# The inner layer's columns dealt in pairs: longer runs for w_out, stepped weight loads for w_in

## The chip, the cores and the metric

The kernel runs on one core of one Trainium2 chip. The metric is the device time of one execution in microseconds, the median of several runs. A core has five engines that work side by side and meet through semaphores: TensorE (matmuls; its weight loads, LDWEIGHTS, are listed apart as PEld), VectorE (DVE), ScalarE (ACT), GpSimd (POOL) and SyncE (SP), which here issues nearly all DMA transfers. Data lies in HBM, is worked on in SBUF (128 partitions), and TensorE writes its sums to PSUM, of which the kernel uses eight banks of 512 float32 columns.

## What is computed

Two layers in a row, float32 in and out. The first is linear attention over 8 batches, 8 heads, 576 positions and 64 features:

```python
q_s = softmax of q over the 64 features
k_s = softmax of k over the 576 positions
kv  = einsum('bhsd,bhse->bhde', k_s, v)   # a 64 x 64 matrix for each head
out = q_s @ kv                             # (8, 8, 576, 64)
x   = out, heads side by side              # 4608 tokens x 512
```

The second is a feed-forward layer with 512 inputs, 2048 inner columns and 512 outputs:

```python
h = x @ w_in                               # w_in 512 x 2048
g = h * (1.0 / (1.0 + np.exp(-beta * h)))  # beta: one value for each of the 2048 inner columns
return g @ w_out                           # w_out 2048 x 512
```

The sum over the 2048 inner columns in the last line may be taken in any order, and it may be cut into any groups, as long as the column of w_in, the value of beta and the row of w_out that belong together meet. The change below is about how these columns are grouped.

## The kernel before

**Chunks and units.** The 4608 tokens are worked through in nine chunks of 512 tokens (`NCH = 9`); chunk 7 is made of the last positions of all batches (`TAILS`), the others of the first 512 positions of one batch. The 2048 inner columns are cut into 16 groups of 128 (`NJ = 16`). A unit `n` is one group `u = n % 16` of one chunk `c = n // 16`; there are 144 units. Each has four steps:

- `h n` (`st1`, line 889): four matmuls of TensorE, one for each 128 rows of w_in. The stationary operand (the weights) is a block of `w_in_b`, 128 x 128, and the moving one is the chunk's `xT`, 512 tokens. They add up in one PSUM bank of a ring of four, `hT`.
- `th n` (`tanh`, line 907): ScalarE takes the tanh, scaled by a column of `beta_c`, which holds one value of beta for each partition.
- `g n` (`gate`, line 924): VectorE computes (tanh + 1) * h into `g`, in bfloat16.
- `o n` (`st2`, lines 951 and 959): four matmuls, one for each 128 tokens. Here `g` is the stationary operand and row group `u` of `w_out_b` the moving one; the results add up over the 16 units of a chunk in four PSUM banks, `acc`, and are stored at its end.

The first four units are cut in halves of 256 tokens, and each half into two pieces of two matmuls (`h 0 0 0` is unit 0, first half, rows 0 and 2 of the four), so that they can start on the first half of `xT`. So the first 32 matmuls of line 889 are 256 columns wide, the others 512.

**Weights.** w_in and w_out come as float32 by DMA into four staging tiles `wst` and are cast to bfloat16 into `w_in_b` and `w_out_b`. There are eight blocks, alternately of w_in (512 of its columns) and of w_out (512 of its rows), each loaded in two halves (`ld w0 1`, `ld w0 0`, ...; `load_w`, lines 316 and 318). The staging tiles are used twice, so that the loads of blocks 4 to 7 wait for the casts of blocks 0 to 3. In a load of w_in each partition gets two runs of 512 values (2 KB), and so it does in one of w_out: row `128 j + p` goes to partition `p`. The casts (`cast_w`, which goes through the helper at lines 232 and 234) are given to ScalarE or GpSimd by the written order. The first block of w_in is cast in two pieces for each half: columns 0 to 127, which is what unit 0 needs, and columns 128 to 511. ScalarE has both pieces of half 1 and the first piece of half 0; GpSimd has the second piece of half 0.

**beta** (lines 343 to 353) is loaded as 16 rows of 128 values, turned by one transpose on TensorE into 128 x 16, and copied to `beta_c` by ScalarE.

**The order.** Every engine works through its instructions in the order in which they are written. That order is the text `ORDER` at the head of the file: 1,200-odd steps, by name, with the engine behind the name where there is a choice. The part that the change touches, the end of the start-up, reads:

```python
kv_0_1, qsum_0_2_0, kexp_0_1, kv_0_0, cast_w0_1_1=act,
qtrev_0_0_0=act, qtr_0_1_0, qmax_1_1, qtrev_0_0_1=dve, qsum_0_2_1, qmax_1_0, cast_w0_1_0=act, ld_w2_0,
qtrev_0_1_0=act, kvn_0, qnorm_0_1_1=pool, cast_w0_0_1=pool, beta_tr, beta_ev, qtr_0_1_1, qsub_1_0=pool,
cast_w0_0_0=act, x_0_0_1, x_0_0_0, qtrev_0_1_1=dve, xev_0_0_0=dve, qrcp_0_2, x_0_1_1, qnorm_0_2_0=pool,
qnorm_0_2_1=pool, xev_0_0_1=act, x_0_1_0, fill_10, fill_5, cast_w2_0=pool, ld_w2_1, xev_0_1_0=dve, ld_w1_0, ld_w1_1,
cast_w2_1=pool, h_0_0_0, h_0_0_1, h_1_0_0, h_1_0_1, h_0_1_0, xev_0_1_1=act, th_0_0, th_1_0, h_0_1_1, qmax_1_2,
```

Here `qtr` are transposes of the normalised q on TensorE, `qtrev` the copies of their results to `qT`, `kv` and `kvn` the 64 x 64 matrices and their normalisation, `x` the matmuls that give x transposed (64 x 64 tiles), `xev` the copies of it to `xT`, and `fill` matmuls whose results nobody uses. The attention of the later batches is woven between the units of the feed-forward layer in the same text. Tiles and semaphores are managed below this level: an instruction waits for those whose data it needs.

Of the kernel before, what the change touches and what calls it, by code (L numbers as in the profile page):

```python
# [9 lines left out]
F32 = mybir.dt.float32  # L10
ALU = mybir.AluOpType
ACTF = mybir.ActivationFunctionType
# [105 lines left out]
def kernel(  # L118
# [11 lines left out]
    P = 128  # L130
# [7 lines left out]
    NJ = FF // P  # L138
# [13 lines left out]
    def op(name, fn, eng=None):  # L152
        assert name not in ops, name
        ops[name] = (fn, eng)
# [4 lines left out]
    def sbt(name, shape, dt):  # L159
        return sb.tile(shape, dt, name=name)  # L160

    ident_f = sbt("ident_f", [P, P], F32)
# [2 lines left out]
    minus = sbt("minus", [P, P], F32)  # L165
    warm = sbt("warm", [P, P], BF16)
    first = sbt("first", [P, 1], F32)
    beta_rows = sbt("beta_rows", [NJ, P], F32)
    beta_c = sbt("beta_c", [P, NJ], F32)
    w_in_b = sbt("w_in_b", [P, KT, FF], BF16)  # L170
    w_out_b = sbt("w_out_b", [P, NJ, DM], BF16)
# [23 lines left out]
    th = [sbt(f"th{i}", [P, 512], BF16) for i in range(3)]  # L195
# [5 lines left out]
    place = {}  # L201
# [4 lines left out]
    def take(*who):  # L206
        assert sum(last in done for last, _ in turns) >= len(who), who
        for w in who:
            n = next(n for n, (last, _) in enumerate(turns) if last in done)
            i = turns.pop(n)[1]  # L210
            place[w] = ring[i][:]
            turns.append((w, i))

    def made(what, *parts):
        done.update((what, p) for p in parts)

    def uses(what, *parts):
        for p in parts:
            assert (what, p) in done, (what, p)
# [7 lines left out]
    dve, act, pool, pe, sp = nc.vector, nc.scalar, nc.gpsimd, nc.tensor, nc.sync  # L227
# [64 lines left out]
    for b in range(B):  # L292
        n = 2 if b else 1
# [4 lines left out]

    W = [(w, blk) for blk in range(4) for w in ("i", "o")]
    w_in_v = w_in.rearrange("(kt p) f -> p kt f", p=P)
    w_out_v = w_out.rearrange("(j p) f -> p j f", p=P)

    def load_w(n, half):
        which, blk = W[n]
        if n > 3:
            which, blk = W[n - 4]
            if which == "i":
                uses("i", *[(4 * blk + u, half) for u in range(4)])  # L310
            else:
                uses("o", 2 * blk + half)
            which, blk = W[n]
        dst = wst[n % 4][:, 2 * half : 2 * half + 2, :]
        if which == "i":
            sp.dma_start(dst, w_in_v[:, 2 * half : 2 * half + 2, 512 * blk : 512 * blk + 512])
        else:
            sp.dma_start(dst, w_out_v[:, 4 * blk + 2 * half : 4 * blk + 2 * half + 2, :])

    def cast_w(n, half, eng, c0=0, c1=512):  # L320
        which, blk = W[n]
        s = wst[n % 4][:, 2 * half : 2 * half + 2, c0:c1]
        if which == "i":
            made("i", *[(4 * blk + c // P, half) for c in range(c0, c1, P)])
            cast(eng, w_in_b[:, 2 * half : 2 * half + 2, 512 * blk + c0 : 512 * blk + c1], s)
        else:
            made("o", 2 * blk + half)
            cast(eng, w_out_b[:, 4 * blk + 2 * half : 4 * blk + 2 * half + 2, :], s)

    for n in range(8):  # L330
        for half in range(2):
            op(f"ld w{n} {half}", lambda n=n, half=half: load_w(n, half))
            if n == 0:
                for c, (c0, c1) in enumerate(((0, P), (P, 512))):
                    op(
                        f"cast w{n} {half} {c}",
                        lambda e, n=n, half=half, c0=c0, c1=c1: cast_w(n, half, e, c0, c1),
                        "pool",
                    )
            else:  # L340
                op(f"cast w{n} {half}", lambda e, n=n, half=half: cast_w(n, half, e), "pool")

    def beta_tr():
        take("beta")
        pe.transpose(place["beta"][:, 0:NJ], beta_rows[:], ident_f[0:NJ, 0:NJ])

    def beta_ev():
        done.add("beta")
        act.copy(beta_c[:], place["beta"][:, 0:NJ])

    op("ld beta", lambda: sp.dma_start(beta_rows[:], beta.rearrange("(j p) -> j p", p=P)))
    op("beta tr", beta_tr)
    op("beta ev", beta_ev)

# [427 lines left out]
    for h in range(3):  # L782
        i0, i1 = 4 * h, min(4 * h + 4, NI)
        for J in range(2):
            p = dict(j=2 * J, n=2, i0=i0, i1=i1)
# [57 lines left out]
    def chunk_x(c):  # L843
        if c == TAILS:
            return xTt
        return xT[(c if c < TAILS else c - 1) % 2]

    def halves(h):
        return (0, 1) if h is None else (h,)

    def cols(h):
        return slice(0, 512) if h is None else slice(256 * h, 256 * h + 256)
# [3 lines left out]
    def bank(n, h):  # L856
        key = ("h", n) if h is None else ("hp", n // 2, h)
        if key not in place:
            take(key)
        if h is None:  # L860
            return place[key]
        return place[key][:, 256 * (n % 2) : 256 * (n % 2) + 256]

    def turn(n, h):
        return n if h is None else 2 * (n // 2) + h

    def st1(n, ks=(0, 1, 2, 3), h=None):
        c, u = divmod(n, NJ)
        x = chunk_x(c)
        for kt in ks:  # L870
            uses("i", (u, kt // 2))
            if c == TAILS:
                uses("xTt", *[(b, kt % 2) for b in range(B)])
            else:
                uses("xT", *[(c - (c > TAILS), kt, a) for a in halves(h)])
        if h is not None and n % 2 and ks[0] == 0:
            uses("st1", (n - 1, h))
        if ks[0]:
            uses("begun", (n, h))
        made("begun", (n, h))  # L880
        w = bank(n, h)
        if c == 0 and h is None:
            w = w.rearrange("p (h c) -> p h c", h=2)
        for kt in ks:
            r = x[:, kt, cols(h)]
            if c == 0:
                r = x_first[:, kt % 2, kt // 2]
                r = r if h is None else r[:, h]
            pe.matmul(  # L889
                w,  # L890
                w_in_b[:, kt, u * P : (u + 1) * P],
                r,
                start=(kt == 0),
                stop=(kt == KT - 1),
            )
        if KT - 1 in ks:
            made("st1", *[(n, a) for a in halves(h)])

    def tanh(n, h=None):
        u = n % NJ  # L900
        mates = [n] if h is None else [2 * (n // 2), 2 * (n // 2) + 1]
        uses("st1", *[(m, a) for m in mates for a in halves(h)])
        if turn(n, h) >= 3:
            uses("gated", turn(n, h) - 3)
        made("tanh", *[(n, a) for a in halves(h)])
        c = cols(None if h is None else n % 2)
        act.activation(th[turn(n, h) % 3][:, c], bank(n, h), ACTF.Tanh, scale=beta_c[:, u : u + 1])  # L907

    def gate(n, h=None):
        mates = [n] if h is None else [n, n + 1]  # L910
# [88 lines left out]
    for n in range(NU):  # L999
        if n < LEAD:  # L1000
            for h in range(2):
                for x in range(2):
                    op(f"h {n} {h} {x}", lambda n=n, h=h, x=x: st1(n, (x, x + 2), h))
                op(f"th {n} {h}", lambda n=n, h=h: tanh(n, h))
                if n % 2 == 0:
                    op(f"g {n} {h}", lambda n=n, h=h: gate(n, h))
                op(f"o {n} {h}", lambda n=n, h=h: st2(n, h))
            continue
        if n in (16, 17):
            op(f"h {n} 0", lambda n=n: st1(n, (0, 1)))  # L1010
            op(f"h {n} 1", lambda n=n: st1(n, (2, 3)))
        else:
            op(f"h {n}", lambda n=n: st1(n))
        op(f"th {n}", lambda n=n: tanh(n))
        op(f"g {n}", lambda n=n: gate(n))
        if n >= NU - LAST:
            for t in range(3):
                op(f"o {n} {t}", lambda n=n, t=t: st2(n, ts=[t]))
            for x in range(2):
                op(f"o {n} 3 {x}", lambda n=n, x=x: st2(n, ts=[3], xs=[x]))  # L1020
        else:
            op(f"o {n}", lambda n=n: st2(n))
# [47 lines left out]
```

## Time and profile before

| | |
|---|---|
| Median of 3 runs (lowest, highest) | 287.05 us (286.97, 287.06) |
| The profiled execution: its own time, its span | 287.31 us, 285.5 us |
| Granted TensorE clock, mean | 0.999 |
| Busy: TensorE, weight loads, VectorE, ScalarE, GpSimd | 275.8, 129.9, 194.9, 174.2, 131.2 us |
| HBM read, written | 36.71 MB, 9.44 MB |
| Loads of w_in: number, size each, median from issue to landing | 8, 512 KB, 7.9 us |
| Loads of w_out: the same | 8, 512 KB, 11.2 us |

Times in the profile are in microseconds from the start of the span. An engine is busy while one of its instructions runs; a row of the profile names the line, the engine, the operation, the tile written and the tile read (`w_in_b<-wst` is a cast of weights), and the shape as partitions x elements. Matmuls are pipelined: one starts before the one ahead of it has left the array, so the length of a single matmul (some 379 ns for 512 columns) is more than the distance between two. Weight loads run beside the matmul ahead. The chain of waits is followed back from the last instruction: at each step it goes to what released it. A wait for several things is put down to the one that came last.

### The profile page before, as it was taken

What the parts mean: (1) busy time and instruction counts of PE and PEld (TensorE: products, weight loads), DVE (VectorE), ACT (ScalarE), POOL (GpSimd) and SP (SyncE); (2) the same over time, 40 slices, a digit from 0 to 9 for tenths busy, and PEclk for the clock granted to TensorE, in tenths of its full rate; (3) what the DMA queues carried; (4) which work ended last, traced back from release to release, by engine and by line L of the source; (5) the groups of instructions that cost most, each with busy time, mean ns of one, the idle gap of its engine ahead of it and who ended that gap; (6) DMA issues with size and microseconds to landing.
All of it is one profiled execution on the core that took longest, in us unless ns stands there. A gap on an engine that the chain in (4) does not pass through costs nothing.

```text
span 285.5 us, 5163 instructions
## 1 busy us (share of the span) xinstructions
PE 275.8 (97%) x1947; PEld 129.9 (45%) x1977; DVE 194.9 (68%) x394; ACT 174.2 (61%) x291; POOL 131.2 (46%) x93
## 2 busy tenths in 40 slices
PE   7799999999999999999999999999999999999994
PEld 2356544444444544444444544444444444444442
DVE  2998957999899898997667858555754263435421
ACT  2498885887488577837586566564671274345422
POOL 6899996869379948083960650090020000000000
PEclk9999999999999999999999999999999999999999
DMA  7999999990991994991434927000054001005104
GB/s 229 390 391 385 384 389 391 390 336 7 276 371 43 316 275 181 295 329 41 152 119 113 189 62 193 0 3 2 0 141 164 0 0 39 0 0 187 73 0 147
DMA packets 37048, 50.01 MB, mean 175 GB/s; under 512 B 15760, under 2 KB 16160, under 8 KB 37024
## 3 DMA queue, kind: packets, MB, share of 16 engines
q1 hardware_dynamic: 36880, 49.63, 53.4%
q8 instruction: 15, 0.25, 0.3%
q10 hardware_dynamic: 144, 0.07, 0.1%
q14 instruction: 9, 0.07, 0.1%
HBM read 36.71 MB, written 9.44 MB: 162 GB/s over the span
## 4 chain that ended last, share of the span: by engine, by line
PE 91%; DMA 4%; ACT 1%; SPq 1%; issue 1%; DVE 0%
PE hT L889 43%; PE acc L959 42%; DMA kf<-in_k_dram 2%; DMA wst<-in_moe_w_in_dram 2%; PE hT L638 2%; PE hT L688 1%; SPq L275 1%; PE hT L951 1%; PE acc L951 1%; ACT w_in_b L232 0%; PE hT L464 0%; PE hT L734 0%; ACT qT L232 0%; ACT ek L612 0%; ACT ek L605 0%
## 5 line engine op out<-in xcount | busy, mean ns | idle before, releaser
L907 ACT ACTIVATE th<-hT,beta_c 128x512 bf16<-128x512 f32 (+1 forms) x148 | 96.6, 677 | 66.9 <-PE hT L889 48.5
L924 DVE SCALAR_TENSOR_TENSOR g<-th,hT 128x512 bf16<-128x512 bf16 x144 | 94.6, 680 | 58.5 <-ACT th L907 55.5
L959 PE MATMUL acc<-w_out_b,g 128*128 128x512 bf16 x543 | 130.7, 379 | 1.4 <-issue 0.8
L889 PE MATMUL hT<-xT,w_in_b 128*128 128x512 bf16 (+1 forms) x517 | 117.7, 372 | 0.7 <-issue 0.2
L889 PEld LDWEIGHTS <-w_in_b 128*128 128x128 bf16 x592 | 57.6, 98 | 64.8 <-ACT w_in_b L232 0.2
L959 PEld LDWEIGHTS <-g 128*128 128x128 bf16 x560 | 53.7, 98 | 64.5 <-issue 2.9
L560 POOL TENSOR_TENSOR kf<-kf,kmb 128x1152 f32<-128x1152 f32 (+1 forms) x15 | 38.0, 2543 | 23.6 <-DVE kmb L550 17.6
L441 POOL TENSOR_TENSOR qn<-eqe,qz 128x1152 bf16<-128x1152 bf16 (+2 forms) x20 | 34.5, 1739 | 28.0 <-DVE qz L433 18.1
L393 POOL TENSOR_TENSOR qf<-qf,qm 128x1152 f32<-128x1152 f32 (+2 forms) x20 | 34.4, 1733 | 18.4 <-issue 11.9
L378 DVE TENSOR_REDUCE qm<-qf 128x9 f32<-128x576 f32 (+2 forms) x34 | 23.3, 704 | 6.2 <-DMA qf<-in_q_dram 6.2
L422 ACT ACTIVATE eqe<-qf 128x576 bf16<-128x576 f32 (+2 forms) x34 | 21.5, 657 | 9.5 <-POOL qf L393 9.5
L232 ACT CAST xT<-hT 128x512 bf16<-128x512 f32 x19 | 12.6, 740 | 21.1 <-PE hT L688 21.1
L428 DVE TENSOR_REDUCE qs<-eqe 128x9 f32<-128x585 bf16 (+2 forms) x34 | 24.0, 713 | 0.5 <-ACT eqe L422 0.4
L490 DVE TRANSPOSE_TENSOR_REDUCE km<-kf 128x18 f32<-128x576 f32 x32 | 23.6, 754 | 0.0
L612 ACT ACTIVATE ek<-kf 128x576 bf16<-128x576 f32 x30 | 19.5, 683 | 0.9 <-DMA vf<-in_v_dram 0.9
L234 POOL CAST va<-vf 128x1152 bf16<-128x1152 f32 (+1 forms) x11 | 12.0, 1105 | 6.9 <-DMA vf<-in_v_dram 6.9
L889 PE MATMUL hT<-xTt,w_in_b 128*128 128x512 bf16 x63 | 14.9, 379 | 0.1
L234 DVE CAST xT<-hT 128x512 bf16<-128x512 f32 x9 | 6.3, 728 | 7.0 <-PE hT L688 7.0
L232 ACT COPY osb<-acc 128x512 f32<-128x512 f32 x14 | 7.8, 594 | 3.0 <-PE acc L959 3.0
L367 PE MATMUL hT<-g,warm 128*128 128x512 bf16 x21 | 7.0, 482 | 1.6 <-POOL g L240 1.5
L234 DVE COPY osb<-acc 128x512 f32<-128x512 f32 (+1 forms) x6 | 3.8, 632 | 4.9 <-PE acc L951 3.8
L638 PEld LDWEIGHTS <-ek 64*64 64x64 bf16 x576 | 5.7, 106 | 2.2 <-issue 1.3
(74 smaller groups left out, 121.7 us busy)
## 6 DMA issues: line engine op xcount, KB each, us to landing
qf<-in_q_dram SPq DMA_DIRECT2D x14, 576.0 KB, 6.9
kf<-in_k_dram SPq DMA_DIRECT2D x14, 576.0 KB, 7.7
vf<-in_v_dram SPq DMA_DIRECT2D x14, 576.0 KB, 8.4
out_dram<-osb SPq DMA_DIRECT2D x19, 256.0 KB, 2.6
wst<-in_moe_w_in_dram SPq DMA_DIRECT2D x8, 512.0 KB, 7.9
wst<-in_moe_w_out_dram SPq DMA_DIRECT2D x8, 512.0 KB, 11.2
out_dram<-wst SPq DMA_DIRECT2D x16, 256.0 KB, 3.7
qf<-in_q_dram SPq DMA_DIRECT2D x4, 288.0 KB, 4.1
```

What stands on the lines that cost most here:

```text
L234: eng.tensor_copy(dst, src)
L378: dve.tensor_reduce(qm[:, j : j + n, i0:i1], qf[b % 2][:, j : j + n, i0:i1], axis=AX.X, op=ALU.max,)
L393: eng.tensor_tensor(x, x, m, ALU.subtract)
L422: act.activation(eq[:, i0:i1, j : j + n, :].rearrange("p i j d -> p j i d"), x, ACTF.Exp)
L428: dve.tensor_reduce(qs[:, i0:i1, j : j + n].unsqueeze(3), x, axis=AX.X, op=ALU.add)
L441: eng.tensor_tensor(qn[b % 2][:, i0:i1, j : j + n, :], eq[:, i0:i1, j : j + n, :], z, ALU.mult)
L490: dve.tensor_reduce(km[:, j : j + n].rearrange("p j i e -> p (j i e)"), kf[b % 2][:, j : j + n].rearrange("p j i (e c) -> p (j i e) c", c=32),
L560: eng.tensor_tensor(x, x, m, ALU.subtract)
L889: pe.matmul(w, w_in_b[:, kt, u * P : (u + 1) * P], r, start=(kt == 0), stop=(kt == KT - 1),)
L907: act.activation(th[turn(n, h) % 3][:, c], bank(n, h), ACTF.Tanh, scale=beta_c[:, u : u + 1])
L924: dve.scalar_tensor_tensor(out=out, in0=of, scalar=1.0, in1=src, op0=ALU.add, op1=ALU.mult)
L959: pe.matmul(acc[t][:], g[n % NG][:, t * P : (t + 1) * P], w_out_b[:, u, :], start=(u == 0), stop=(u == NJ - 1),)
```

## The change

Inner columns are dealt to the units in pairs. Two neighbouring units `2m` and `2m + 1` share the 256 columns from `256 m` on; the first takes the even ones and the second the odd ones, so that partition `p` of unit `2m + r` is column `256 m + 2 p + r`. Before, unit `u` took columns `128 u` to `128 u + 127`.

- **w_out**: rows `256 m + 2 p` and `256 m + 2 p + 1` go to the same partition and lie side by side in HBM, so that a load has one run of 4 KB for each partition in place of two of 2 KB. The tile `w_out_b` and the matmuls that read it are as before.
- **w_in**: loads and layout in SBUF are as before. The weight load of a unit now takes every second of 256 columns, a step of two elements. The two pieces of the first block are columns 0 to 255 and 256 to 511, since units 0 and 1 need the first 256.
- **beta**: loaded as 8 rows of 256 values; two transposes, one for the even and one for the odd values (read with a step of two), in place of one. `beta_c` has the even units in its first eight columns and the odd ones in the other eight, and `tanh` picks the column by `v`.

The number and order of all other instructions are the same.

```diff
-    beta_rows = sbt("beta_rows", [NJ, P], F32)
+    beta_rows = sbt("beta_rows", [NJ // 2, 2 * P], F32)
...
-    w_out_v = w_out.rearrange("(j p) f -> p j f", p=P)
+    w_out_v = w_out.rearrange("(m p r) f -> p m r f", p=P, r=2)
...
-            sp.dma_start(dst, w_out_v[:, 4 * blk + 2 * half : 4 * blk + 2 * half + 2, :])
+            sp.dma_start(dst, w_out_v[:, 2 * blk + half])
...
-                for c, (c0, c1) in enumerate(((0, P), (P, 512))):
+                for c, (c0, c1) in enumerate(((0, 2 * P), (2 * P, 512))):
...
-        pe.transpose(place["beta"][:, 0:NJ], beta_rows[:], ident_f[0:NJ, 0:NJ])
+        for r in range(2):
+            n = NJ // 2
+            pe.transpose(place["beta"][:, n * r : n * r + n], beta_rows[:, r : 2 * P : 2], ident_f[0:n, 0:n])
...
-    op("ld beta", lambda: sp.dma_start(beta_rows[:], beta.rearrange("(j p) -> j p", p=P)))
+    op("ld beta", lambda: sp.dma_start(beta_rows[:], beta.rearrange("(m q) -> m q", q=2 * P)))
...
-                w_in_b[:, kt, u * P : (u + 1) * P],
+                w_in_b[:, kt, 2 * P * (u // 2) + u % 2 : 2 * P * (u // 2) + 2 * P : 2],
...
         u = n % NJ
+        v = NJ // 2 * (u % 2) + u // 2
...
-        act.activation(th[turn(n, h) % 3][:, c], bank(n, h), ACTF.Tanh, scale=beta_c[:, u : u + 1])
+        act.activation(th[turn(n, h) % 3][:, c], bank(n, h), ACTF.Tanh, scale=beta_c[:, v : v + 1])
```

## The prediction

> **What bounds the kernel now.** I read the page first (busy shares, the chain), then the busy time of each engine over the long middle, then what TensorE waits for there, then the start-up instruction by instruction. From the page:
>
> ```profile
> PE 275.8 (97%) x1947; PEld 129.9 (45%) x1977; DVE 194.9 (68%) x394; ACT 174.2 (61%) x291; POOL 131.2 (46%) x93
> ...
> PE 91%; DMA 4%; ACT 1%; SPq 1%; issue 1%; DVE 0%
> ```
>
> TensorE is busy 275.8 of 285.5 us and holds 91% of the chain. Next, busy time by engine from the first matmul of the inner layer to 262 us (from, to, length, then busy us and instructions by engine, granted clock, share of the DMA engines, GB/s), and all waits of TensorE from 20.5 us to the end:
>
> ```profile
> 20.57:262.00 241.43, 239.37 (x1695) 111.73 (x1721) 173.71 (x346) 155.27 (x257) 114.95 (x64) 1.00 0.53 169
> ```
>
> ```profile
> PE acc L959 <- issue: 0.8, 5, 0.2
> PE hT L367 <- issue: 0.2, 1, 0.2
> PE hT L889 <- issue: 0.2, 1, 0.2
> ```
>
> In 241.43 us TensorE is idle for 2.06, at a granted clock of 1.00, and no wait is on a DMA, a cast or another engine; they are 0.2 us each, where it comes back from 64x64 tiles to full ones. So the time is three things: when the inner layer starts (20.57 us), how fast matmuls follow one another, and the end. A change counts if it moves the start or the pitch. The chain of waits, in order of time (start, length, what), shows both:
>
> ```profile
> 4.03 6.47 DMA kf<-in_k_dram
> ...
> 10.52 5.99 DMA wst<-in_moe_w_in_dram
> ...
> 17.67 0.72 ACT w_in_b L232
> 18.39 0.36 ACT qT L232
> ...
> 18.76 0.42 ACT w_in_b L232
> 19.18 0.49 ACT qT L232
> ...
> 19.72 0.41 PE acc L688 x8
> 20.13 0.16 issue
> 20.29 0.38 PE hT L367
> 20.67 7.01 PE hT L889 x48
> ...
> 37.32 3.46 PE hT L889 x16
> ```
>
> Sixteen 512-column matmuls of L889 take 3.46 us, 0.216 each. Ahead of the first one ScalarE is the chain: it alternates the first w_in casts with copies of qT. The change touches these casts.
>
> **The first w_in casts.** Two units now share 256 columns, so the first 512-column block is cut 256 + 256 in place of 128 + 384. On ScalarE the order stays: rest of half 1, qT, first part of half 1, qT, beta, first part of half 0, then the first xT copy. GpSimd has the rest of half 0. ScalarE's timeline (start, length, instruction):
>
> ```profile
> 17.56 0.83 ACT L232 CAST w_in_b<-wst 128x768 bf16<-128x768 f32 x1
> 18.28 0.59 ACT L232 COPY qT<-acc 128x512 bf16<-128x512 bf16 x1
> 18.76 0.42 ACT L232 CAST w_in_b<-wst 128x256 bf16<-128x256 f32 x1
> ...
> 19.07 0.60 ACT L232 COPY qT<-acc 128x512 bf16<-128x512 bf16 x1
> 19.54 0.20 ACT L349 COPY beta_c<-hT 128x16 f32<-128x16 f32 x1
> 19.61 0.44 ACT L232 CAST w_in_b<-wst 128x256 bf16<-128x256 f32 x1
> 19.91 0.77 ACT L232 CAST xT<-acc 128x512 bf16<-128x512 f32 x1
> ```
>
> 768 values a partition take 0.83 us and 256 take 0.42: 0.41 for 512 values, so 512 take 0.42 + 0.205 = 0.63. The first cast shrinks by 0.20, the second grows by 0.20: the qT copy of 19.07 starts when it did. The third, of 19.61, also grows, and nothing pays for it: 0.44 becomes 0.64, and the xT copy behind it moves from 19.91 to 20.12 and ends at 20.89, not 20.68. Who waits for it is TensorE's third matmul. Its rows, with VectorE's xT copy, which lets the first one go:
>
> ```profile
> 20.29 0.38 PE L367 MATMUL hT<-g,warm 128*128 128x512 bf16 x1 [0.16 <-issue]
> 20.57 0.49 PE L889 MATMUL hT<-xT,w_in_b 128*128 128x256 bf16 x3
> ```
>
> ```profile
> 19.77 0.75 DVE L234 CAST xT<-acc 128x512 bf16<-128x512 f32 x1 [0.22 <-ACT beta_c L349]
> ```
>
> VectorE ends at 20.52 and the first matmul starts at 20.57: 0.05 for the hand-over. One 256-column matmul lasts 0.27 (row below), so the third of 20.57 to 21.06 starts at 20.79. ScalarE's copy was ready for it at 20.68 + 0.05 = 20.73, 0.06 ahead. With 20.89 + 0.05 = 20.94 it starts 0.15 late. The next copy (second of its kind) then ends near 21.50, ahead of its matmul, the eleventh: 20.57 + 10 x 0.109 + 0.15 = 21.81. So the stream loses **0.15 us**, once. Bounds: 0, if the cast overlaps the copy, and 0.2, the whole growth. I take 0.15 since each link has its own row. GpSimd's 0.82 us cast of 768 shrinks by some 0.2; it moves up a chain that TensorE doesn't wait for: no gain.
>
> **beta by two transposes.** One weight load and one matmul of fp32 more:
>
> ```profile
> 18.46 0.13 PEld L345 LDWEIGHTS hT<-ident_f,beta_rows 16*128 16x128 f32 x1
> 18.62 0.17 PEld L464 LDWEIGHTS <-qn 128*128 128x128 bf16 x3
> ...
> 18.46 0.23 PE L345 MATMUL hT<-ident_f,beta_rows 16*128 16x16 f32 x1
> ```
>
> From its load to the next load is 0.16 us; that is the price of the second. Queued behind it on TensorE are four transposes, which VectorE's copy of qT waits for, and then the second x matmuls, which end at 20.13 by the chain; they move by 0.16 at most. So do the two fill matmuls behind them. The last fill could let L889 start at 20.29 + 0.22 = 20.51, and it starts at 20.57, so that 0.06 are free and the first two matmuls of L889 move by at most 0.1, still ahead of 20.94. ScalarE reads beta only at 19.54, 0.85 us after the transpose ends. Cost: 0 under the cover of the late xT copy; with that cover gone up to 0.1. The beta load (8 runs of 1 KB for 16 of 512 B) stands in SP's queue ahead of the w_in loads, which were cast from 17.56 on: it is in time.
>
> **w_in's weights with a step of two.** The main risk: 592 weight loads of L889. Rows by shape (busy us, mean ns, idle before), and from the timeline eight loads and transposes in a row, and the kv loads:
>
> ```profile
> L889 PE MATMUL hT<-xT,w_in_b 128*128 128x256 bf16 x32 | 3.7, 273 | 0.0
> ...
> L889 PEld LDWEIGHTS <-w_in_b 128*128 128x128 bf16 x592 | 57.6, 98 | 64.8 <-ACT w_in_b L232 0.2 <-issue 0.2
> ...
> L580 PEld LDWEIGHTS acc<-kf,ident_f 128*128 128x128 f32 x4 | 0.7, 188 | 1.3 <-issue 1.2
> ```
>
> ```profile
> 17.24 0.85 PEld L638 LDWEIGHTS <-ek 64*64 64x64 bf16 x72 [0.46 <-ACT ek L612]
> ...
> 31.94 0.61 PE L464 MATMUL hT<-ident,qn 128*128 128x128 bf16 x8
> ```
>
> A load takes 98 ns from start to end, under a matmul with a pitch of 216 (109 in the 32 of 256 columns). Back to back they go closer: eight transposes, each with its load, take 0.61 us, (0.61 - 0.22) / 7 = 0.056 a load. No load of before has a step, so its price is bounded: from below 0 (a load already hidden can't gain); from above by the fp32 load, 188 ns, whose 128 columns lie four bytes apart, as the stepped ones do. The 64-column loads of L638 say that even narrow ones go at 0.85 us for 18 at each of four tile positions, under 0.05 each, so 128 columns under 0.1. All of these are under 0.216, and 560 of 592 loads are hidden whichever holds. Exposed would be the 32 with a pitch of 0.109 and the three units (31, 51, 109) that the written order puts right behind 64x64 work. At 0.188: 31 x (0.188 - 0.109) = 2.4 and 3 x 0.09 = 0.3, so **+2.7 us** as the upper end. I take 0: nearest are the bf16 rows, 0.056 to 0.1, under both pitches.
>
> Here a rule speaks against the change. The Trainium skill, "TensorE: Matmul & The Clock Gate", section "Weight-path perf modes — Fast Weight Load (FWL) and DoubleRow", says that a full bf16 load reads 32 bits, two weights, at a time in four chunks, packed or stepped. By it, as an estimate, a step of two would waste half of each read; no load of before can show that. The same page's plain formula (columns / 1.2 ns) gives 107 ns, under 109. What half the rate would cost from rows is a rival below.
>
> **w_out in runs of 4 KB.** Eight loads; half as many packets each. The rows (size, median us from issue to landing), then all traffic at 14 to 17 us (nearly all w_in, runs of 2 KB) and at 44 to 56 us (q, k, v, runs of 2.25 KB):
>
> ```profile
> wst<-in_moe_w_out_dram SPq DMA_DIRECT2D x8, 512.0 KB, 11.2
> ```
>
> ```profile
> DMA packets 587, 1.17 MB, mean 391 GB/s; under 512 B 32, under 2 KB 32, under 8 KB 587
> ```
>
> ```profile
> DMA packets 2178, 4.68 MB, mean 390 GB/s; under 512 B 128, under 2 KB 128, under 8 KB 2176
> ```
>
> 391 against 390 GB/s: the queue is full and the longer run is no faster. At 390 a load of 0.52 MB is 1.34 us of the stream. Runs of 4 KB may save some of that, at most 8 x 1.34 = 10.7, likely under 1; but no TensorE wait after 20.5 is on a DMA, and the chain's DMA pieces, k and w_in, end at 16.51. The closest use is the first w_out block:
>
> ```profile
> 26.07 2.02 POOL L234 CAST w_out_b<-wst 128x1024 bf16<-128x1024 f32 x2
> ...
> 27.52 1.89 PE L959 MATMUL acc<-w_out_b,g 128*128 128x512 bf16 x7
> ```
>
> Half of it is cast at 27.08 and used at 27.52: 0.4 us of room, and GpSimd was held by its own queue, not the load. Cost and gain 0. SP's next w_in load waits for the longer cast of 19.61 and so goes out 0.2 us later, into a queue that stays full: 0. If that cover went, 0.2 more.
>
> **Sum.** +0.15 (cast) + 0 + 0 + 0 on the profiled span of 285.5: 285.65. That run took 287.31 (1.8 around the span), 0.26 above the median of 287.05; on the median, 287.05 + 0.15 = **287.20**.
>
> **Rivals.** (a) Stepped loads at half rate: 0.112 each against 0.109: 31 x 0.003 + 3 x 0.06 = 0.3, so 287.5. For it: the rule above; against: nothing measured. (b) Slower side: stepped loads as slow as fp32 ones. Place: the 32 half-width matmuls from 20.57 on. It decides from 0.109 us a load; price 2.7, so 289.9. Above 0.216 every unit would pay, 560 x the excess, for which no row speaks. (c) A cast or copy with little room (0.06 to 0.4 us) arrives late because the start-up shifts ScalarE, GpSimd and VectorE against each other: a new wait of 0.5 to 1, so 287.7 to 288.2. Against it: they follow TensorE's own shift. (d) Faster: the shorter DMA stream brings everything forward. It needs a TensorE wait on data, and there is none after 20.5; before it, at most 0.2 from the shorter first cast: 286.85. (e) Long runs change nothing in the queue, landing still near 11.2: the time is that of my sum.
>
> **Chances.** My sum, with (e): 0.72, own range 287.0 to 287.45. (a) 0.10, (b) 0.07, (c) 0.07, (d) 0.04. The range from 286.8 to 288.2 leaves out (b) and odd cases. 0.2% is 0.57 us, about what a measurement here can tell from no change: 286.48 to 287.62. Within it are my sum, nearly all of (a), and a quarter of (d): 0.82; slower: (b), (c) and 0.01 of (a), 0.15; faster: the rest of (d), 0.03, for a wait in the start-up that is worth more than I can see.
>
> **What would show it.** The third L889 matmul at 20.94, 0.15 late; the cast ahead of xT at 0.63; two loads of beta 0.1 to 0.16 apart; L889's 512-column matmuls at 0.216 still, the 256-column ones at 0.109; the w_out packets halved and no DMA wait on TensorE. Wrong if L889's weight loads rise over 109 ns with the pitch following, or a new wait of TensorE shows between 20 and 60 us.

## The result: 3% slower, and the profile after

The changed kernel takes 295.5 us (median; lowest 294.0, highest 297.53) against 287.01 before, a ratio of 1.030 (95% interval 1.024 to 1.0365). The profiled execution took 294.0 us with a span of 292.2; before it was 287.31 and 285.5. From the page of the changed kernel, the busy times, the chain and the granted clock in 40 slices of 7.3 us:

```profile
PE 277.2 (95%) x1948; PEld 130.5 (45%) x1978; DVE 195.1 (67%) x394; ACT 175.0 (60%) x291; POOL 131.1 (45%) x93
...
PEclk9999979999999999999999999999999999999999
...
PE 86%; DMA 4%; DVE 3%; issue 2%; POOL 1%; ACT 1%; SPq 1%; DVEq 0%; POOLq 0%
```

TensorE is busy for 1.4 us longer, with one matmul more on the page, and its share of the span falls from 97% to 95%; GpSimd, which was not in the chain before, has a share of it, and in one slice the granted clock falls. Whom TensorE waited for, from 18 us to the end (us in total, times, longest):

```profile
PE hT L892 <- POOL w_in_b L234: 5.6, 3, 3.2
PE acc L963 <- issue: 0.8, 5, 0.2
PE hT L892 <- issue: 0.2, 1, 0.2
PE hT L370 <- issue: 0.2, 1, 0.2
```

Three rows of before are there again. New are three waits of the inner layer's matmuls (line 892 is 889 before) for casts of w_in on GpSimd. TensorE's timeline at these places, and GpSimd's (start, length, instruction):

```profile
19.48 0.38 PE L892 MATMUL hT<-xT,w_in_b 128*128 128x256 bf16 x2
21.55 0.28 PE L892 MATMUL hT<-xT,w_in_b 128*128 128x256 bf16 x1 [1.69 <-POOL w_in_b L234]
22.54 0.72 PE L892 MATMUL hT<-xT,w_in_b 128*128 128x256 bf16 x5 [0.70 <-POOL w_in_b L234]
...
34.04 0.38 PE L892 MATMUL hT<-xT,w_in_b 128*128 128x512 bf16 x1
37.64 2.63 PE L892 MATMUL hT<-xT,w_in_b 128*128 128x512 bf16 x7 [3.22 <-POOL w_in_b L234]
40.07 1.06 PE L467 MATMUL hT<-ident,qn 128*128 128x128 bf16 x8
```

```profile
20.46 2.02 POOL L234 CAST w_in_b<-wst 128x1024 bf16<-128x1024 f32 x2
...
36.54 1.04 POOL L234 CAST w_in_b<-wst 128x1024 bf16<-128x1024 f32 x1
```

The first two matmuls of unit 0 run; the third starts when the first of GpSimd's two casts of 20.46 is through, the fourth when the second is, at 22.48. By the written order these are the casts of block 1, the columns 512 to 1023, and unit 0 reads columns 0 to 255. Unit 10 is held in the same way: its first matmul runs at 34.04, its second waits until the cast of 36.54, which is block 3, columns 1536 to 2047, has ended at 37.58; unit 10 reads 1280 to 1535. TensorE waits for data that it doesn't use, so the section on the kernel before, where an instruction waits for those whose data it needs, is not the whole truth. In the kernel before, the same cast of block 3 starts when unit 10 is already through: its four matmuls are the first of eight in a row, without a wait:

```profile
32.39 1.89 PE L889 MATMUL hT<-xT,w_in_b 128*128 128x512 bf16 x8
...
34.88 1.04 POOL L234 CAST w_in_b<-wst 128x1024 bf16<-128x1024 f32 x1
```

Behind the last wait the seven matmuls take 2.63 us, where six distances of 0.216 and one length of 0.38 make 1.68. The busy times in stretches (from, to, length, busy us by engine, then granted clock, DMA share and GB/s), of the changed kernel:

```profile
34.00:42.00 8.00, 4.78 (x24) 2.30 (x22) 4.70 (x12) 3.60 (x5) 7.31 (x6) 0.79 1.04 393
...
37.60:41.70 4.10, 4.06 (x17) 2.04 (x18) 1.24 (x3) 1.91 (x3) 3.43 (x2) 0.58 1.04 395
```

In the kernel before, the stretch from 34 to 42 has TensorE busy for 7.95 of 8.00 us at a clock of 1.00, against 4.78 at 0.79 here:

```profile
34.00:42.00 8.00, 7.95 (x44) 3.95 (x44) 5.42 (x14) 7.10 (x11) 7.30 (x5) 1.00 1.05 388
```

So the span of the profiled execution adds up. The matmul behind each wait starts 1.96, 0.99 and 3.60 us after the one ahead of it, where 0.109, 0.109 and 0.216 were due: 1.85 + 0.88 + 3.38 = 6.1 lost. The clock costs 4.10 x (1 - 0.58) = 1.7. The inner layer started at 19.48, 1.1 earlier than at 20.57 before; that start lies between 19.20 and 20.73 in the profiles of this document, so the 1.1 is not put down to the change. 6.1 + 1.7 - 1.1 = 6.7, which is 292.2 - 285.5.

The profiled execution is the fastest of the four, and the clock accounts for the others. Their spans are 292.2, 293.7, 295.7 and 293.7 us at mean granted clocks of 0.992, 0.988, 0.981 and 0.988; span times clock is 289.9, 290.2, 290.1 and 290.2.

### The profile page after: what moved, and what is told of

The parts are those of the page before. It is cut to its first block, busy times and chain, and to the rows that moved or that the text cites. A ratio compares the mean times of both kernels' runs of the same rounds, so it can differ in the third digit from the quotient of the medians.

```text
span 292.2 us, 5166 instructions
## 1 busy us (share of the span) xinstructions
PE 277.2 (95%) x1948; PEld 130.5 (45%) x1978; DVE 195.1 (67%) x394; ACT 175.0 (60%) x291; POOL 131.1 (45%) x93
## 4 chain that ended last, share of the span: by engine, by line
PE 86%; DMA 4%; DVE 3%; issue 2%; POOL 1%; ACT 1%; SPq 1%; DVEq 0%; POOLq 0%
PE hT L892 40%; PE acc L963 40%; DMA kf<-in_k_dram 3%; PE hT L641 2%; DMA qf<-in_q_dram 1%; PE hT L691 1%; DVE km L493 1%; POOL qn L444 1%; DVE qs L431 1%; PE hT L955 1%; PE acc L955 1%; PE acc L596 1%; SPq L275 1%; DVE qm L381 1%; ACT th L911 1%
## 5 line engine op out<-in xcount | busy, mean ns | idle before, releaser
L892 PE MATMUL hT<-xT,w_in_b 128*128 128x512 bf16 (+1 forms) x517 | 119.5, 375 | 6.3 <-POOL w_in_b L234 5.6
```

The costliest lines, as they stand in the source:

```text
L892: pe.matmul(w, w_in_b[:, kt, 2 * P * (u // 2) + u % 2 : 2 * P * (u // 2) + 2 * P : 2], r, start=(kt == 0), stop=(kt == KT - 1),)
```

## The experiments

Two theories that stood against each other, and a third. **W**: a stepped load is made to wait for casts of other columns, since tiles are watched for overlap, and a load with a step of two and a cast of two rows in one tile are held to overlap although they share no element. **S**: the stepped loads themselves are slow, or disturb what runs beside them. **R**: the 4 KB runs change when weights land. Intervals are of 95%.

### The same stepped loads, with w_in in several tiles

```diff
-    w_in_b = sbt("w_in_b", [P, KT, FF], BF16)
+    w_in_0 = [[sbt(f"w_in_0_{a}_{c}", [P, 2, 256], BF16) for c in range(2)] for a in range(2)]
+    w_in_t = [[sbt(f"w_in_{blk}_{a}", [P, 2, 512], BF16) for a in range(2)] for blk in range(1, 4)]
...
-                w_in_b[:, kt, 2 * P * (u // 2) + u % 2 : 2 * P * (u // 2) + 2 * P : 2],
+                w_in_of(u // 4, kt // 2, 256 * (u // 2 % 2))[:, kt % 2, u % 2 : 2 * P : 2],
```

> The changed kernel with w_in_b cut into several tiles: the first block into one tile for each half and 256 columns, the other blocks into one for each half. All 592 weight loads keep their step of two, w_out keeps its 4 KB runs, beta its two transposes. Theory W (a stepped load is made to wait for GpSimd casts of columns that it doesn't read, since casts of two rows of w_in and the stepped columns are held to overlap in one tile): no wait for a cast at units 0 and 10, no stretch at a lower clock behind it, 287.0 to 287.5 us. Rival S (the stepped loads themselves are slow or disturb TensorE): 294 to 297 us as in the changed kernel. Rival R (the 4 KB runs change when weights land): 294 to 297 us.

Measured: 287.5 us, ratio 1.0006 (0.9995 to 1.0018). TensorE waits for nothing behind 18 us. Two stretches of its profile, and its rows of the inner layer by shape (busy us, mean ns, idle before):

```profile
20.73:34.00 13.27, 13.27 (x86) 7.80 (x85) 12.17 (x22) 11.48 (x23) 12.03 (x11) 1.00 1.04 393
34.00:42.00 8.00, 8.00 (x44) 3.86 (x43) 5.54 (x14) 7.08 (x12) 7.31 (x6) 1.00 1.03 397
```

```profile
L899 PE MATMUL hT<-xT,w_in 128*128 128x256 bf16 x32 | 3.8, 272 | 0.0
...
L899 PEld LDWEIGHTS <-w_in 128*128 128x128 bf16 x592 | 57.6, 98 | 64.9 <-ACT w_in L239 0.2 <-issue 0.2
```

All that the change does to loads, runs and beta is still there, and the loss is gone. S and R fall. A stepped load takes 98 ns, as a contiguous one did, in the same 57.6 us for 592.

### Five stepped loads in the kernel before

```diff
-                w_in_b[:, kt, u * P : (u + 1) * P],
+                (w_in_b[:, kt, 2 * P * (u // 2) + u % 2 : 2 * P * (u // 2) + 2 * P : 2]
+                 if (u, kt) in ((0, 1), (0, 3), (10, 1)) and n < NJ else w_in_b[:, kt, u * P : (u + 1) * P]),
```

> The kernel before, in which only the weight loads of unit 0 (rows 1 and 3 of the four) and unit 10 (row 1) take every second column: five of 592 load instructions. These units then use other columns of w_in than they should, so two of the 2048/128 groups of the first chunk are computed with mixed columns. All else is before: 2 KB runs, one transpose of beta, contiguous loads. Theory W: those are the loads that get the waits, so the time is that of the changed kernel, 294 to 297.5 us, with three waits of TensorE on GpSimd casts of 5 to 6.5 us in total. Rival S: 5 slow loads cost under 1 us, 287.0 to 288.0 us. Rival R: 287.0 us.

Measured: 296.8 us, ratio 1.033 (1.0312 to 1.0348). Five of 592 loads give the whole loss, with three waits of the same total:

```profile
PE hT L889 <- POOL w_in_b L234: 5.8, 3, 3.2
```

Here the clock fell behind the early waits too, and the profiled run took 297.05 us:

```profile
PEclk9997989999999999999999999999999999999999
```

### The changed kernel without the step; the long runs alone

The first edit gives line 892 its contiguous slice back and keeps everything else of the change:

```diff
-                w_in_b[:, kt, 2 * P * (u // 2) + u % 2 : 2 * P * (u // 2) + 2 * P : 2],
+                w_in_b[:, kt, u * P : (u + 1) * P],
```

> The changed kernel with contiguous weight loads of w_in, as before: 4 KB runs, two transposes of beta and the first block's casts of 256 + 256 columns stay. Columns of w_in then meet other values of beta and other rows of w_out than they should, which changes the result and no instruction. Theory W and rival S: 287.0 to 287.4 us, the difference to before being what the longer cast ahead of the first xT copy costs (0.15 us by the prediction's sum). Rival R: 294 to 297 us.

Measured: 287.18 us, ratio 1.0001 (0.9988 to 1.0014). The second takes the kernel before and changes w_out alone:

```diff
-    w_out_v = w_out.rearrange("(j p) f -> p j f", p=P)
+    w_out_v = w_out.rearrange("(m p r) f -> p m r f", p=P, r=2)
...
-            sp.dma_start(dst, w_out_v[:, 4 * blk + 2 * half : 4 * blk + 2 * half + 2, :])
+            sp.dma_start(dst, w_out_v[:, 2 * blk + half])
```

> The kernel before with w_out loaded in 4 KB runs and nothing else changed; the rows of w_out then meet other columns than they should, which changes the result and no instruction. Theory W and rival S: 287.0 us within 0.2, no TensorE wait on a DMA or a cast, and the median from issue to landing of the w_out loads tells what 4 KB runs do to the queue. Rival R: some us slower, with a wait on a cast of weights.

Measured: 287.01 us, ratio 0.9993 (0.9979 to 1.0008), no wait of TensorE behind 18 us. Its packets and its w_out loads, and then the packets of the kernel before:

```profile
DMA packets 36024, 50.01 MB, mean 175 GB/s; under 512 B 15760, under 2 KB 16160, under 8 KB 36000
...
wst<-in_moe_w_out_dram SPq DMA_DIRECT2D x8, 512.0 KB, 10.7
```

```profile
DMA packets 37048, 50.01 MB, mean 175 GB/s; under 512 B 15760, under 2 KB 16160, under 8 KB 37024
```

1024 packets fewer than the 37048 of before, as 8 x 128 should give, and the median from issue to landing is 10.7 us against 11.2, at the same mean rate. In the other runs here in which TensorE is not held up it is 10.5, 9.7 and 10.6 with the long runs (the changed kernel without the step, and the two with several tiles) and 11.1 with the short ones (the run of rows 0 and 2, below). With the loads hidden, neither shows in the time. R falls a second time. Beta and the casts cost nothing that these intervals tell from no change; their 0.15 us is looked for below in the trace.

### Which stepped loads are held back

> The kernel before with a step of two in the weight loads of rows 0 and 2 of the four (296 of 592), the other loads contiguous; the sums then mix columns of w_in that don't belong together. Theory W in a sharper form: a stepped load is held against the stretch from the first to the last element of a cast, and a cast covers columns of two rows in one tile, so that its stretch takes in the other columns of the second row (rows 1 and 3), not those of the first (rows 0 and 2). Then none of these loads gets a wrong wait: no TensorE wait on a cast behind the start, 287.1 us within 0.5. If any stepped load gets such waits, or if the step costs time in itself: 290 us or more.

```diff
-                w_in_b[:, kt, u * P : (u + 1) * P],
+                (w_in_b[:, kt, 2 * P * (u // 2) + u % 2 : 2 * P * (u // 2) + 2 * P : 2]
+                 if kt % 2 == 0 else w_in_b[:, kt, u * P : (u + 1) * P]),
```

Measured: 287.21 us, ratio 1.0001 (0.998 to 1.0021); TensorE's waits are the three `issue` rows of before, and the clock doesn't fall. So 296 stepped loads cost nothing, and one of unit 10 costs 5 us (below). That bears out the sharper form of W. In a partition, w_in_b holds four rows of 2048 elements. The cast of block 3, half 0, writes columns 1536 to 2047 of rows 0 and 1, that is, elements 1536 to 2047 and 3584 to 4095. Unit 10, row 1, lies at 3328 to 3583: between the two pieces, inside the stretch from first to last. Row 0 lies at 1280 to 1535, outside. By this reading the pieces are told apart for a contiguous load, and for a stepped one only the stretch is looked at. It was put down ahead of this run and fits every wait that came and every one that did not; the code that sets the waits was not looked into, so the rule itself is inferred.

### The two places alone

> The kernel before with a step of two in the loads of unit 0, rows 1 and 3, alone (four of 592 load instructions); unit 0 then reads other columns of w_in than it should. Theory W: the two early waits (1.85 and 0.88 us in the changed kernel) and nothing at unit 10: 287.1 + 2.7 = 289.8 us; should the waits also bring a stretch at half the clock, as one did in the run with five stepped loads, up to 1.8 more, 291.6. If the loss belonged to the stretch at unit 10 alone: 287.1.

> The kernel before with a step of two in one load, that of unit 10, row 1; unit 10 of the first chunk then reads other columns than it should. Theory W: one wait of 3.4 us near 34 us, and behind it matmuls 0.427 us apart for some 3.4 us, which cost 1.7: 287.1 + 5.1 = 292.2 us, within 0.7. Rival (the loss needs many stepped loads): 287.1.

Both are the edit above with another condition:

```diff
-                 if kt % 2 == 0 else
+                 if (u, kt) in ((0, 1), (0, 3)) and n < NJ else
```

```diff
-                 if kt % 2 == 0 else
+                 if (u, kt) == (10, 1) and n < NJ else
```

Measured: 291.23 us, ratio 1.0145 (1.0128 to 1.0162), and 292.24 us, ratio 1.0165 (1.014 to 1.019): 4.2 and 5.2 us more than before. Together 9.4, against 9.7 of the run with both. TensorE at unit 0, and its clock behind it:

```profile
22.83 0.28 PE L889 MATMUL hT<-xT,w_in_b 128*128 128x256 bf16 x1 [1.89 <-POOL w_in_b L234]
23.81 3.45 PE L889 MATMUL hT<-xT,w_in_b 128*128 128x256 bf16 x17 [0.70 <-POOL w_in_b L234]
```

```profile
23.90:26.80 2.90, 2.90 (x15) 1.98 (x16) 0.77 (x2) 0.84 (x2) 0.00 (x0) 0.51 1.05 388
```

At a clock of 0.51, 17 matmuls of 256 columns take 3.45 us; 16 x 0.109 + 0.28 would be 2.02, so the clock costs 1.4 here, beside 2.9 of waiting. At unit 10:

```profile
36.11 3.17 PE L889 MATMUL hT<-xT,w_in_b 128*128 128x512 bf16 x7 [3.21 <-POOL w_in_b L234]
```

```profile
36.10:39.30 3.20, 3.19 (x10) 1.26 (x11) 1.21 (x3) 0.69 (x1) 2.56 (x2) 0.50 1.05 389
```

3.20 x (1 - 0.50) = 1.6, beside 3.4 of waiting.

### Filling the wait

```diff
+            for _ in range(16 if (n, kt) == (10, 1) else 0):
+                pe.matmul(w, warm[:], r, start=False, stop=False)
             pe.matmul(
```

> The changed kernel with 16 matmuls with weights of zero ahead of the load of unit 10, row 1, which add nothing to its sum and take 16 x 0.216 = 3.46 us, about as long as TensorE stands still there. If the lower clock behind that wait comes from TensorE's standing still: the wait is filled, the stretch at 0.427 us a matmul goes, and the time falls by 1.7, to 293.8 us (292.3 to 295.8 as the changed kernel varies). If the clock falls for another reason: 295.5, or more.

Measured: 294.2 us, ratio 1.0254 (1.023 to 1.0277). The 16 idle matmuls take the place of the wait, and the seven behind them run at full speed:

```profile
35.15 3.62 PE L893 MATMUL hT<-xT,warm 128*128 128x512 bf16 x16
38.60 1.67 PE L894 MATMUL hT<-xT,w_in_b 128*128 128x512 bf16 x7
```

The stretch around them, columns as above:

```profile
34.00:42.00 8.00, 7.95 (x49) 4.10 (x49) 5.59 (x15) 3.97 (x6) 7.25 (x6) 1.00 1.04 394
```

1.67 us for seven, not 2.63, at a clock of 1.00: what lowers the clock is that TensorE stands still. In the three profiles with the same wait unfilled (the changed kernel, five stepped loads, unit 10 alone) the clock fell each time. The median falls by 1.3 us where 1.7 were expected; the intervals of the two ratios overlap (up to 1.0277 here, from 1.024 there), so that the trace shows this, and the times alone would not. Two of the four executions have a mean granted clock of 1.000 (293.35 and 293.68 us) and two of 0.993 and 0.994 (294.73 and 294.93 us): the early waits are still there, but the last two were not profiled, so that where the clock fell in them stays open.

### The late third matmul

This one is made from the kernel with several tiles, and moves one cast in the written order (the rest of the lines is left out):

```diff
-... kv_0_0, cast_w0_1_1=act,
+... kv_0_0,
...
-... cast_w0_0_1=pool, beta_tr, ...
+... cast_w0_0_1=pool, cast_w0_1_1=pool, beta_tr, ...
```

> The changed kernel with w_in_b in several tiles, as in the run of that kind, and the first of ScalarE's three casts of w_in's first block (the rest of half 1) given to GpSimd, behind the rest of half 0. By the prediction's sum the 0.15 us that the third matmul of the inner layer came late (0.264 us behind the second, not 0.109) come from the longer cast ahead of the first xT copy; with 0.63 us less on ScalarE ahead of it the gap closes: the third matmul 0.109 behind the second, and 0.15 us less than with the cast on ScalarE, 287.1 us, equal to before. GpSimd is 0.6 later with its next steps, which TensorE needs only from 24 us on: no new wait.

Measured: 287.31 us, ratio 1.0003 (0.999 to 1.0016), against 1.0006 with the cast on ScalarE. In the trace the third matmul is on time. The first matmuls of the inner layer, first with the cast on ScalarE, then on GpSimd:

```profile
20.73 0.64 PE L899 MATMUL hT<-xT,w_in 128*128 128x256 bf16 x3
```

```profile
19.20 0.60 PE L899 MATMUL hT<-xT,w_in 128*128 128x256 bf16 x4
```

Three take 0.64 us with the longer cast, 0.49 in the kernel before, and four take 0.60 = 3 x 0.109 + 0.27 with the cast moved. So the 0.15 us is real in the trace; it is under what these times can tell. No version here beats the kernel before.

## Why the prediction was wrong

**The step that failed** is the term "w_in's weights with a step of two", of which the prediction says "I take 0", and with it the sum of 287.20 and the upper end of 288.2. It priced the load and asked whether it is hidden. It did not ask what each load waits for once its slice has a step. Two loads of unit 0 and one of unit 10 got a wait that the contiguous slice does not have, worth 6.1 us, and standing still cost 1.7 to 3 more in clock. The prediction went by the written order, which is the same in both kernels; the waits are not written there.

**The price of a stepped load was right**: 98 ns, and the 256-column matmuls keep their distance of 0.109 (four in 0.60 us). Rival (b), loads as slow as fp32 ones, is out. Rival (a), half the rate, could not be seen at all in the distances of the 32 narrow matmuls, which would have grown by 0.003 each; but the length of a load didn't grow either. The Trainium skill, "SBUF — State Buffer", section "Door 1: The DMA port swizzle", says that consecutive reads from one line of 16 bytes go at full rate if a line is hit at least twice; at a step of two a line still gives four bf16 weights, and the measured 98 ns agrees. The half rate that the prediction estimated from another page, the Trainium skill, "TensorE: Matmul & The Clock Gate", section "Weight-path perf modes — Fast Weight Load (FWL) and DoubleRow", does not show.

**Rival (c)**, a new wait in the start-up, came nearest, for another reason and at about a tenth of the size: it looked for casts that come late, and these casts came no later than TensorE's own shift made them (the first pair 0.98 us behind the first inner matmul, 1.18 before). What it would look like was named: "a new wait of TensorE shows between 20 and 60 us".

**The cast term was right.** Predicted: the third matmul 0.15 late; measured: 0.15, in the kernel without the false waits (three in 0.64 us, not 0.49).

**beta** was right as a cost under cover. In the run with several tiles the pair of transposes starts at 18.62 and the next work at 18.95:

```profile
18.62 0.40 PE L355 MATMUL hT<-ident_f,beta_rows 8*128 8x8 f32 x2
18.95 0.40 PE L474 MATMUL acc<-ident,qn 128*128 128x128 bf16 x4
```

0.33 us, where one took 0.16: 0.17 for the second, 0.16 predicted. Nobody waits for it.

**w_out** was right in the time: half the packets and no effect. Rival (e) had the landing still near 11.2; it came sooner, at 9.7 to 10.7, where nothing held TensorE up.

**The clock** was no step of the prediction, since nothing was to stand still. That a gap on TensorE can be paid for twice belongs to the price of any new wait.

## What to carry to other kernels

When a slice that an instruction reads or writes changes its step or its bounds, list what each instruction waits for, before and after: a framework that finds waits from overlaps may know less about a stepped slice than about a contiguous one, and the order of instructions alone doesn't show it. Where a stepped operand is wanted, cut the tile along the lines at which its producers write it; here that gave back all of the 8.5 us. On a TensorE that is busy without a gap, count a new wait of some us at up to one and a half times its length (2.9 + 1.4 and 3.4 + 1.6 us above).

## What the runs showed of the hardware

Two things that I had not expected. Weight loads of 128 bf16 columns with a step of two cost the same 98 ns as contiguous ones. For the fp32 loads of beta, read at eight bytes a column, no price of the step is shown: they take 202 ns, where the one before took 133, but over 8 rows and not 16, contiguous fp32 loads take 188, and each still takes 0.16 to 0.17 us of TensorE's time, as the one before did:

```profile
L348 PEld LDWEIGHTS hT<-ident_f,beta_rows 8*128 8x128 f32 x2 | 0.3, 202 | 0.1
```

And a TensorE that has stood still for 2 to 3 us can run at half its clock for the next 3.4 us. Read in windows of 0.1 us, the clock is 0.50 from 38.22 to 41.64 us in the changed kernel, from 24.35 to 27.76 and from 41.42 to 44.83 in the run with five stepped loads, from 23.34 to 26.76 and from 35.86 to 39.27 in the runs of unit 0 and unit 10 alone: 3.41 us each time, and in the run with both, the second fall comes 17.07 us, five times 3.41, behind the first. Whether a wait brings it on varies: those of 1.9 and 0.7 us at unit 0, with one matmul between them, did in the profiles of the two runs made from the kernel before, and those of 1.7 and 0.7 did not in those of the changed kernel and of the run with the wait filled. It seems to hang on how the wait lies against steps of 3.41 us. In the step ahead of each of the five falls TensorE stands still for 2.3 to 3.0 us; steps counted back from the fall in the changed kernel part its two early waits, with 1.6 us of standing still in one and 1.1 in the next, and the clock stays at 1.00. That is a reading of five falls; no run tested it.

The Trainium skill, "TensorE: Matmul & The Clock Gate", section "Part 1: The HAM clock gate (the "warmup" mystery)", has the clock at half after an idle window of about 3.4 us whose phase runs on by itself. The traces agree in the half, in the length and in the phase; but 2.3 us of standing still in such a window were enough here.
